# Moving the products of v's sums with w_in behind the output product in an attention and ELU layer kernel

## The chip, the cores and the metric

The kernel runs on one core of one Trainium2 chip. The metric is the device time of one execution in microseconds (us), as the median of the runs; lower is better.

## The reference

Two parts follow each other. The first is an attention with 32 memory slots: phi (8 batches, 8 heads, 576 positions, 32 slots) gives weights over positions, with which k and v are summed into 32 slots per head; q then attends to the slots. The second takes the result, 512 values for each of 4608 tokens, through w_in, an ELU and w_out.

```python
a = phi - np.max(phi, axis=2, keepdims=True)
a = np.exp(a)
a = a / (np.sum(a, axis=2, keepdims=True) + 1e-09)
k_m = np.einsum('bhsm,bhsd->bhmd', a, k)
v_m = np.einsum('bhsm,bhsd->bhmd', a, v)
...
scores = scale * np.matmul(q, k_m.transpose(0, 1, 3, 2))
...
attn = attn / (np.sum(attn, axis=-1, keepdims=True) + 1e-09)
return np.matmul(attn, v_m).astype(np.float32)
...
h = x @ w_in
g = np.where(h > 0.0, h, alpha * (np.exp(np.minimum(h, 0.0)) - 1.0))
return (g @ w_out).astype(np.float32)
```

The inputs are float32, w_in is 512 x 2048, w_out 2048 x 512.

## The kernel before, in words

The kernel never forms the attention's output. It multiplies v's sums of a batch with w_in first (`vw`, line 594), a small product per head, and then the probabilities A with that result. In the profile the product is line L502, which writes psb and reads win and kvm; L502 with qt in place of win is the score product. The product of one batch comes in four parts, one for each block of 512 columns of w_in; the text calls them the products with the first to the fourth block.

Each such product fills two accumulator banks named psb, of which there are two in all; the sums over positions (`slots`, L453), their transposes (`slots_transpose`, L487) and the scores use the same two in turn. ScalarE copies each bank as a high part into the tile vw (`vw_high`, L605), and VectorE writes the remainder as a low part (`vw_low`, L611). A bank is free once its low part is written.

The main loop runs over 256 steps `it`, each a batch b, a half hf of its positions (288) and a chunk j of 128 of the 2048 channels. A step has:

- `hidden` (L657, psh <- A, vw), six matmuls into one of two banks psh: the *channel product*;
- the ELU: two ScalarE passes (`elu_exp`, L672 and L673, into gf), and on VectorE the maximum (`elu_max`, L684, and L686 for the 32 rest columns), after which the psh bank is free;
- the split into a high part (`elu_high`, L698, ScalarE) and a low part (`elu_low`, L704, VectorE) in the tile gp;
- `project` (L712, pso <- wout, gp), six matmuls into two banks that collect a half's output over 16 chunks: the *output product*.

The channel product of a step stands two steps ahead of its output product. So TensorE's queue is channel product, output product, channel product, output product, and the work of the next batch's attention is placed in between.

The order is set by places: `at(place, f, ...)` records a step, and the list is sorted by place. `hidden` of step it has place it - 1.7, `project` it + 0.6, so between two whole steps n and n+1 the places are n + 0.3 for a channel product and n + 0.6 for an output product. For batches 2 to 7, `products(b, c, o)` (line 828) puts the product of batch b with block c at o, its high part at o + 0.75 and its low part at o + 0.76. `attention(b, o)` places the rest: phi's maximum and its way through DRAM to all partitions (`spread_max`, tiles nmd and nmb), the shift of e by it on GpSimd (`e_shift`, L289) and the exponential on ScalarE (`e_exp`, L294), the sums, their transposes at o + 7.2 and the copy of the transposes (`kv_copy`, L494, tile kvm). For batches 0 and 1 and the start of batch 2 the order is a table written out by hand (`FIRST`), which includes the products of batch 2 with its first two blocks. 22 products are left for the plan.

The recorded order is kept as it is on TensorE and for SyncE's transfers. On ScalarE, VectorE and GpSimd, outside the hand-written table, the framework's scheduler sets the order. All engines run their queues in order.

The batch's attention is placed against the batch ahead of it: the transposes of batch b's sums stand shortly behind the product of batch b-1 with its fourth block, and the shifts and exponentials of e of batch b shortly behind that of batch b-1 with its third block. When a pair of batches is done, the columns left over from the halves (288 = 2 x 128 + 32) are put through w_out together (`rest_project`, also L712, and the copy `rest_store`, L771).

## Time and profile before

| what | value |
|---|---|
| median of 3 runs | 736.43 us (736.42 to 736.93) |
| the profiled execution | 735.4 us, its span 733.6 us |
| TensorE matmul busy | 709.2 us of the span |
| VectorE busy | 467.2 us |
| ScalarE busy | 465.0 us |
| GpSimd busy | 44.6 us |
| mean granted TensorE clock | 0.990 |

The profile is one execution. Its times count from the first instruction. In rows of the timeline the first number is the start, the second the time from there to the end of the group, then the engine (PE is TensorE, PEld its weight loads, DVE VectorE, ACT ScalarE, POOL GpSimd, SP SyncE), the line of the kernel, the operation, what it writes and reads by the program's names, and in brackets how long the engine was idle just before and on what it waited. Matmuls overlap and their ends are modelled, so the time of a block of matmuls is read from its start to the start of the next block. A row may hold several instructions (x6).

### The profile page before, as it was taken

The page shows a single profiled execution, that of the slowest core. Times are in us where ns is not written, and L with a number is a line of the kernel's source. Part 1 is how long each engine was busy: PE and PEld are TensorE (multiplying, and loading weights), DVE is VectorE, ACT ScalarE, POOL GpSimd, SP SyncE. Part 2 cuts the span into 40 slices and gives each one's busy share as a digit, 9 for nine tenths or more (in the row PEclk, how much of TensorE's full clock was granted, in tenths as well). Part 3 has the DMA queues.
Part 4 walks back from the last instruction along what each step waited for, and adds up shares of the span by engine and source line. Part 5 has one row for each costly group of instructions (what it writes and reads, how often), then busy time and mean ns, then how long its engine had stood idle before and what let it go on. Part 6 is the DMA issues. An engine that isn't in the chain of part 4 may idle for free.

```text
span 733.6 us, 13668 instructions
## 1 busy us (share of the span) xinstructions
PE 709.2 (97%) x5114; PEld 572.5 (78%) x5114; DVE 467.2 (64%) x1253; ACT 465.0 (63%) x1110; POOL 44.6 (6%) x88
## 2 busy tenths in 40 slices
PE   7688999999999999999999999999999999999997
PEld 6566888888768878877788777887787887888885
DVE  4999899886495467544954449545774447754442
ACT  4768988886456656755655557656565565665552
POOL 0001112123000100010000100000000010000000
PEclk9899999999999999999999999999999999999999
DMA  8960513431316110611015210260002600010002
GB/s 311 370 231 28 203 30 115 149 101 62 101 59 210 28 44 1 239 42 45 2 57 182 56 45 1 75 206 28 18 1 75 218 27 20 1 58 0 2 1 72
DMA packets 24978, 64.46 MB, mean 88 GB/s; under 512 B 3408, under 2 KB 7632, under 8 KB 24912
## 3 DMA queue, kind: packets, MB, share of 16 engines
q1 hardware_dynamic: 24912, 63.59, 25.7%
q8 instruction: 41, 0.67, 0.4%
q14 instruction: 25, 0.20, 0.1%
HBM read 54.13 MB, written 9.44 MB: 87 GB/s over the span
## 4 chain that ended last, share of the span: by engine, by line
PE 68%; DMA 14%; DVE 8%; ACT 5%; issue 2%; POOL 1%; SPq 1%; POOLq 0%; DVEq 0%; ACTq 0%
PE pso L712 41%; PE psh L657 21%; DMA nmd<-nm 6%; PE psb L502 4%; DMA nmb<-nmd 3%; PE psb L453 2%; DMA ph<-phiT 2%; POOL e L289 1%; DMA win<-w_in 1%; ACT gf L673 1%; DMA kvt<-kv 1%; ACT gf L672 1%; DMA e<-phi 1%; DVE gf L681 1%; DVE nm L407 1%
## 5 line engine op out<-in xcount | busy, mean ns | idle before, releaser
L712 PE MATMUL pso<-wout,gp 128*128 128x512 f32 x1728 | 449.6, 398 | 3.3 <-DVE gp L704 2.6
L712 PEld LDWEIGHTS pso<-wout,gp 128*128 128x128 f32 x1728 | 310.1, 188 | 84.2 <-ACT gf L673 13.0
L657 PEld LDWEIGHTS psh<-A,vw 128*128 128x128 f32 x1536 | 229.9, 189 | 39.5 <-issue 6.2
L657 PE MATMUL psh<-A,vw 128*128 128x288 f32 x1536 | 251.1, 299 | 8.6 <-DVE rest L686 3.8
L684 DVE SCALAR_TENSOR_TENSOR gf<-gf,psh 128x256 f32<-128x256 f32 x192 | 80.4, 419 | 130.3 <-ACT gf L673 130.0
L672 ACT ACTIVATE gf<-psh 128x288 f32<-128x288 f32 x256 | 104.7, 409 | 86.3 <-PE psh L657 84.4
L698 ACT CAST gp<-gf 128x256 fp32r<-128x256 f32 x256 | 103.4, 404 | 87.0 <-DVE gf L684 73.4
L704 DVE TENSOR_TENSOR gp<-gf,gp 128x256 fp32r<-128x256 f32 x256 | 107.6, 421 | 55.0 <-ACT gp L698 54.7
L673 ACT ACTIVATE gf<-gf 128x288 f32<-128x288 f32 x256 | 113.7, 444 | 7.8
L611 DVE TENSOR_TENSOR vw<-psb,vw 128x512 fp32r<-128x512 f32 (+2 forms) x74 | 43.3, 602 | 11.7 <-ACT vw L605 11.5
L289 POOL TENSOR_TENSOR e<-e,nmb 128x512 f32<-128x512 f32 (+1 forms) x18 | 19.7, 1122 | 377.1 <-DMA nmb<-nmd 374.8
L681 DVE SCALAR_TENSOR_TENSOR gf<-gf,psh 128x288 f32<-128x288 f32 x64 | 28.9, 452 | 18.2 <-ACT gf L673 16.9
L605 ACT CAST vw<-psb 128x512 fp32r<-128x512 f32 (+2 forms) x74 | 37.1, 522 | 2.9 <-PE psb L502 0.7
L502 PE MATMUL psb<-win,kvm 64*32 64x512 f32 (+2 forms) x592 | 36.0, 541 | 0.0
L694 POOL COPY rest<-gf 128x32 f32<-128x32 f32 x64 | 24.3, 380 | 167.6 <-DVE gf L681 167.5
L686 DVE SCALAR_TENSOR_TENSOR rest<-gf,psh 128x32 f32<-128x32 f32 x192 | 34.2, 179 | 0.1
L752 ACT CAST gp<-rest 128x256 fp32r<-128x256 f32 x32 | 13.0, 406 | 23.8 <-PE pso L712 21.8
L373 DVE SCALAR_TENSOR_TENSOR top<-mag,top 128x512 uint32<-128x512 uint32 x32 | 22.2, 692 | 1.9 <-ACT mag L364 0.3
L757 DVE TENSOR_TENSOR gp<-rest,gp 128x256 fp32r<-128x256 f32 x32 | 13.4, 418 | 15.0 <-ACT gp L752 14.9
L368 ACT ACTIVATE mag<-raw 128x512 uint32<-128x512 uint32 x30 | 20.0, 670 | 2.5 <-DVE top L373 2.5
L294 ACT ACTIVATE e<-e 128x512 f32<-128x512 f32 (+1 forms) x18 | 9.8, 559 | 16.9 <-POOL e L289 16.8
L364 ACT ACTIVATE mag<-raw 128x512 f32<-128x512 f32 x30 | 19.5, 668 | 0.4 <-DVE win L385 0.4
(96 smaller groups left out, 368.4 us busy)
## 6 DMA issues: line engine op xcount, KB each, us to landing
kvt<-kv SPq DMA_DIRECT2D x32, 512.0 KB, 7.4
out<-osb SPq DMA_DIRECT2D x16, 512.0 KB, 2.8
raw<-w_in SPq DMA_DIRECT2D x15, 512.0 KB, 6.0
raw<-w_out SPq DMA_DIRECT2D x15, 512.0 KB, 7.9
qt<-q SPq DMA_DIRECT2D x18, 384.0 KB, 4.3
ph<-phiT SPq DMA_DIRECT2D x7, 576.0 KB, 5.0
e<-phi SPq DMA_DIRECT2D x12, 256.0 KB, 6.3
qh<-q SPq DMA_DIRECT2D x4, 576.0 KB, 11.5
```

The costliest lines, as they stand in the source:

```text
L502: nc.tensor.matmul(outs[a][32 * j : 32 * j + 32, :], lhs[r, 32 * j : 32 * j + 32], rhs[r, j], start=True, stop=True, tile_position=(64 * a ...
L605: nc.scalar.copy(s["vw"][c][:, HI, a, n0:n1], ps)
L611: nc.vector.tensor_tensor(t[:, LO, a, n0:n1], ps, t[:, HI, a, n0:n1], ALU.subtract)
L657: nc.tensor.matmul(ps, t[:, x, g, c0 : c0 + P], s["A"][hf][:, y, g, :], start=(n == 0), stop=(n == 5),)
L672: nc.scalar.activation(gf, ps, AF.Relu, scale=-1.0)
L673: nc.scalar.activation(gf, gf, AF.Exp, scale=-1.0)
L681: nc.vector.scalar_tensor_tensor(gf, gf, -1.0, ps, ALU.add, ALU.max)
L684: nc.vector.scalar_tensor_tensor(gf[:, :n], gf[:, :n], -1.0, ps[:, :n], ALU.add, ALU.max)
L686: nc.vector.scalar_tensor_tensor(rest_of(b, j)[:, o : o + REST], gf[:, n:], -1.0, ps[:, n:], ALU.add, ALU.max)
L698: nc.scalar.copy(gp[:, HI], gs[it][:, : NT * P])
L704: eng.tensor_tensor(gp[:, LO], gf[:, : NT * P], gp[:, HI], ALU.subtract)
L712: nc.tensor.matmul(ps, gp[:, y], wout[j][:, x, :], start=(first and n == 0), stop=(last and n == 2),)
```

## The change

One number in the plan: the place of the products of batches 2 to 7.

```diff
         attention(b, 43 if b == 2 else base - 22)
         for c in range(NVC):
-            products(b, c, base - 7.6 + 8 * c)
+            products(b, c, base - 7.35 + 8 * c)
```

`base` and 8c are whole numbers. Before, a product stood at a place n + 0.4: behind a channel product (n + 0.3) and ahead of an output product (n + 0.6). Now it stands at n + 0.65: behind that output product and ahead of the next channel product (n + 1.3). Its high and low parts move by the same 0.25, from n + 1.15 to n + 1.40 and from n + 1.16 to n + 1.41. The number of instructions and what they compute stay the same. The orders of SyncE and GpSimd are the same; those of TensorE, ScalarE and VectorE change.

## The prediction

> **What bounds the kernel now.** I read the page first: the busy shares.

> ```profile
> PE 709.2 (97%) x5114; PEld 572.5 (78%) x5114; DVE 467.2 (64%) x1253; ACT 465.0 (63%) x1110; POOL 44.6 (6%) x88
> ```

> TensorE is busy 97% of the span. So a microsecond that TensorE waits is a microsecond of time, and what VectorE and ScalarE do counts only where TensorE comes to wait for it. The change adds no instruction. It has to be priced by two things: what a change of neighbours costs on TensorE, and which waits appear or go.

> The timeline of TensorE alone gives the neighbours' prices: from one block's start to the next block's start is what a block costs. This stretch holds batch 4's product with the third block of w_in (L502, 16 records); L657 are channel products, L712 output products.

> ```profile
> 409.90 0.96 PE L657 MATMUL psh<-A,vw 128*128 128x288 f32 x6
> 410.79 1.09 PE L502 MATMUL psb<-win,kvm 64*32 64x512 f32 x16
> 411.81 1.65 PE L712 MATMUL pso<-wout,gp 128*128 128x512 f32 x6
> 413.30 0.96 PE L657 MATMUL psh<-A,vw 128*128 128x288 f32 x6
> 414.10 1.56 PE L712 MATMUL pso<-wout,gp 128*128 128x512 f32 x6
> 415.50 0.95 PE L657 MATMUL psh<-A,vw 128*128 128x288 f32 x6
> 416.29 0.43 PE L712 MATMUL pso<-wout,gp 128*128 128x512 f32 x1
> 417.02 1.42 PE L712 MATMUL pso<-wout,gp 128*128 128x512 f32 x5 [0.30 <-DVE gp L704]
> 418.95 1.04 PE L657 MATMUL psh<-A,vw 128*128 128x288 f32 x6 [0.51 <-DVE rest L686]
> ```

> An undisturbed channel block takes 0.80 us (413.30 to 414.10) and an output block 1.40 (414.10 to 415.50). With the product between them the channel block takes 0.89, the product 1.02, the output block 1.49. The second thing to see: here TensorE's close row of blocks breaks. The output block of 416.29 is followed by the next channel block only at 418.95, 2.66 us on, 1.26 more than undisturbed. ScalarE's timeline and GpSimd's over the same stretch tell why.

> ```profile
> 411.34 0.44 ACT L673 ACTIVATE gf<-gf 128x288 f32<-128x288 f32 x1
> 414.76 0.63 ACT L294 ACTIVATE e<-e 128x512 f32<-128x512 f32 x1 [2.98 <-POOL e L289]
> 415.30 0.57 ACT L605 CAST vw<-psb 128x512 fp32r<-128x512 f32 x1
> 415.76 0.41 ACT L698 CAST gp<-gf 128x256 fp32r<-128x256 f32 x1
> 416.07 0.59 ACT L605 CAST vw<-psb 128x512 fp32r<-128x512 f32 x1
> 416.55 0.94 ACT L294 ACTIVATE e<-e 128x512 f32<-128x512 f32 x2
> 417.38 0.40 ACT L672 ACTIVATE gf<-psh 128x288 f32<-128x288 f32 x1
> ```

> ```profile
> 413.42 3.26 POOL L289 TENSOR_TENSOR e<-e,nmb 128x512 f32<-128x512 f32 x3 [90.00 <-DMA nmb<-nmd]
> ```

> ScalarE waits 2.98 us for the first of GpSimd's three shifts of e, and everything behind it in its queue comes late: the casts, and then L672, which a channel block needs done before a later one may use its bank again.

> Then the list of who waited for whom (us in all, times, longest), the timeline of TensorE around batch 4's product with the fourth block of w_in, and VectorE's first low part there.

> ```profile
> PEld psb L487 <- DVE vw L611: 1.3, 5, 0.3
> ```

> ```profile
> 432.63 0.95 PE L657 MATMUL psh<-A,vw 128*128 128x288 f32 x6
> 433.51 1.09 PE L502 MATMUL psb<-win,kvm 64*32 64x512 f32 x16
> 434.53 1.66 PE L712 MATMUL pso<-wout,gp 128*128 128x512 f32 x6
> 436.02 0.42 PE L487 MATMUL psb<-ident,x 128*128 128x128 f32 x2
> 436.20 1.04 PE L657 MATMUL psh<-A,vw 128*128 128x288 f32 x6
> 437.08 1.56 PE L712 MATMUL pso<-wout,gp 128*128 128x512 f32 x6
> 438.57 0.56 PE L502 MATMUL psb<-qt,kvm 64*32 64x192 f32 x16
> 439.05 1.07 PE L657 MATMUL psh<-A,vw 128*128 128x288 f32 x6
> 439.97 1.29 PE L712 MATMUL pso<-wout,gp 128*128 128x512 f32 x5
> ```

> ```profile
> 435.26 0.69 DVE L611 TENSOR_TENSOR vw<-psb,vw 128x512 fp32r<-128x512 f32 x1 [0.21 <-ACT vw L605]
> ```

> Five times the weight load of the transposes (L487) waits for VectorE's L611, the low part of the product just before: the transposes write into the bank that L611 empties. Today that wait costs TensorE nothing. The product begins at 433.51, L611 ends at 435.95, the transposes start at 436.02, and until just then the output block (434.53 to 436.02) fills TensorE. That block is the cover.

> **The change, part by part.** All 22 products that the plan places keep their work; each moves behind the output block that followed it.

> (1) The product with the fourth block, five times (batches 2 to 6). TensorE's order at batch 2's, pso being output blocks, psh channel blocks, psb<-win the product, psb<-ident,x the transposes:

> ```order
>  L712 MATMUL pso_2849<-wout_1317,gp 128x512 x3
>  L657 MATMUL psh<-A,vw 128x288 x6
> -L502 MATMUL psb<-win_80,kvm 32x512 x8
>  L712 MATMUL pso_2825<-wout_1591,gp 128x512 x3
>  L712 MATMUL pso_2826<-wout_1591,gp 128x512 x3
> +L502 MATMUL psb<-win_80,kvm 32x512 x8
>  L487 MATMUL psb<-ident,x 128x128 x2
>  L657 MATMUL psh<-A,vw 128x288 x6
> ```

> The output block no longer stands between the product and the transposes, so the cover is gone and the wait is paid in full. From the product's start to the transposes' start it is 2.51 us (433.51 to 436.02), whichever block lies between: both halves must be cast by L605 and L611 before the first bank is free. Before, from the channel block to the next output block: 432.63 to 437.08, 4.45 us. After: channel block 0.80, output block ahead of a tiled product 1.49 (437.08 to 438.57), product and wait 2.51, transposes 0.18 and channel block 0.88 (436.02 to 437.08): 5.86. That is +1.41 each, +7.05 for five. Behind the waiting transposes stand the next channel block and all of TensorE's queue, so nothing fills the gap; ScalarE's and VectorE's ELU work runs dry with it. Bounds: at least 1.41 - 0.11 = 1.30 each if the joint behind the output block (1.49 against 1.40) and the transposes' cost nothing in the new place, at most 1.60 if a cast starts 0.2 late (6.5 to 8.0). L605 now stands behind L698, whose input is an ELU that ends before the product does, so I take no delay from it.

> (2) The product with the third block, five times (batches 2 to 6), where ScalarE waits for e. There the order of ScalarE's queue changes too. Batch 4's, before: L672 and L673 are the ELU's two passes, L698 the cast of its result, L294 the three exponentials of e, L605 the casts of the product.

> ```order
> L673 ACTIVATE gf<-gf 128x288
> L294 ACTIVATE e<-e 128x512
> L605 CAST vw<-psb 128x512
> L698 CAST gp<-gf 128x256
> L605 CAST vw<-psb 128x512
> L294 ACTIVATE e<-e 128x512
> L294 ACTIVATE e<-e 64x256
> L672 ACTIVATE gf<-psh 128x288
> ```

> And with the change:

> ```order
> L673 ACTIVATE gf<-gf 128x288
> L294 ACTIVATE e<-e 128x512 x2
> L698 CAST gp<-gf 128x256
> L294 ACTIVATE e<-e 64x256
> L605 CAST vw<-psb 128x512 x2
> L672 ACTIVATE gf<-psh 128x288
> ```

> The second exponential now stands ahead of L698 and of both casts, and GpSimd gives its input only at about 416.0: the first shift took 1.3 (413.42 to just before 414.76), and so does the second. So after the first exponential (414.76 to 415.39) ScalarE waits again: second exponential 416.03 to 416.66, L698 to 416.98, third exponential to 417.28, the casts L605 from 417.18 to 418.25, L672 from 418.15 where it was 417.38: +0.77. What follows L672 keeps its gaps, and the channel block of 418.95, which waits for the last of it, comes at 419.72. The output block of 416.29 goes on about 0.45 later than now, and ends before that: no further wait. So +0.77 here. Batches 2 and 6 have the same two exponentials ahead of the casts. In batches 3 and 5 the order is another: L672 and L673 stand between the exponentials, and the third exponential, L698 and both L605 ahead of the next L672, where one L605 stood on each side of the third exponential and L698. Batch 5's rows now, ScalarE alone:

> ```profile
> 496.83 0.42 ACT L673 ACTIVATE gf<-gf 128x288 f32<-128x288 f32 x1
> 497.16 0.56 ACT L605 CAST vw<-psb 128x512 fp32r<-128x512 f32 x1
> 497.62 0.41 ACT L294 ACTIVATE e<-e 64x256 f32<-64x256 f32 x1
> 497.94 0.39 ACT L698 CAST gp<-gf 128x256 fp32r<-128x256 f32 x1
> 498.24 0.58 ACT L605 CAST vw<-psb 128x512 fp32r<-128x512 f32 x1
> 498.71 0.41 ACT L672 ACTIVATE gf<-psh 128x288 f32<-128x288 f32 x1
> ```

> With the first cast moved behind L698, the third exponential takes its place at 497.16, and L698 starts at about 497.74 (VectorE's maximum, which it waits for, ends some 0.45 behind L673's end at 497.25). Then the casts at 498.05 and 498.53 and L672 at 499.02: +0.31, and the channel block that waits for it comes about 0.30 later. Sum: 3 x 0.77 + 2 x 0.30 = +2.9. Batches 2, 3 and 6 I take like the two that I worked out. Bounds: 0, if the delay of the exponentials is taken up somewhere behind, and 5 x 1.0, if every place costs batch 4's 0.77 and another 0.2 of a late cast.

> (3) The other 12 products. Before: 0.89 + 1.02 + 1.49 and a channel block of 0.80 behind, 4.20. After: channel 0.80, output 1.49, product 1.02, channel block behind a tiled product 0.91 (439.05 to 439.97, from the score product), 4.22. +0.02 each, +0.2. The casts L605 now follow L698 and precede the next L672; that one's input comes only after the later channel block, so they fit between, and no wait is added. One place needs a look: the product with a batch's second block now stands behind that batch's first output block, which writes a bank that has to be emptied first. The tightest case, behind the rest columns' output, ScalarE's copy and TensorE's channel block:

> ```profile
> 391.18 0.95 PE L657 MATMUL psh<-A,vw 128*128 128x288 f32 x6
> ```

> ```profile
> 391.38 0.59 ACT L771 COPY orest<-pso 128x512 f32<-128x512 f32 x1 [0.99 <-PE pso L712]
> ```

> The copy ends at 391.97, the channel block without its joint at 391.98. So the output block could wait 0.1 at most, at two places; I take nothing.

> SyncE's and GpSimd's orders are unchanged, so no DMA is moved.

> Sum: 7.05 + 2.9 + 0.2 = +10.2. The profiled execution took 735.4 us, its span 733.6; so 745.6 in its terms. The median of the runs shown is 1.0 above it, 736.43, so the forecast is 746.6.

> **Rivals.** (a) ScalarE's new order costs nothing, the transposes' wait is all: 736.4 + 7.2 = 743.7. It needs the exponentials' inputs to come earlier against TensorE; nothing on SyncE or GpSimd does that. Chance 0.10.

> (b) The channel block runs past the waiting transposes, so (1) costs nothing: 736.4 + 3.1 = 739.5. Against it: in the rows above TensorE's blocks start in the order in which they stand. Chance 0.04. [...]

> (c) Not slower: the stall in (2) vanishes altogether at all five places, because the maxima (nmb) land early enough that ScalarE never waits for e. Gain: 1.26 us at batch 4 as read above, so about 6.2 for five if the others are alike (an estimate from that row), against 7.05 + 0.2: 736.4 + 1.1 = 737.5, within what can be told from no change, and under it if the others were larger. It decides once GpSimd's first shift ends by 411.78, where L673 ends, and not just before 414.76: 3 us earlier. Against it: the transfers stand in SyncE's unchanged queue. Chance 0.06.

> (d) The five gaps of 1.5 us make the granted clock fall. The lowest granted clock of any stretch that I read is 0.81, near the start; behind the gap of batch 4 it is 1.00.

> ```profile
> 416.20:419.80 3.60, 2.79 (x14) 1.94 (x14) 2.31 (x6) 3.05 (x8) 0.49 (x1) 1.00 0.00 0
> 18.34:36.68 18.34, 12.38 (x179) 10.08 (x182) 17.72 (x50) 13.90 (x37) 0.42 (x2) 0.81 1.03 370
> ```

> If each gap cost what that stretch lost, 0.19 x 18.3 = 3.5 us, it would add up to 17: 764. Chance 0.03. [...]

> **The numbers.** The forecast has 0.77; its bounds are 736.4 + 6.5 = 742.9 and 736.4 + 8.0 + 5.0 + 0.4 = 749.8. The range 743.2 to 749.0 takes in (a) and leaves out (b), (c), (d) and the outermost of the bounds. A measurement of this kernel can tell about 0.2% (1.5 us) from no change. Of (c)'s 0.06, 0.04 lie within it and 0.02 under it; all else is slower: 0.94.

> **What would show it.** Right: the list of waits shows TensorE's transposes (psb, L487) waiting for VectorE's L611 at some 1.5 us five times; block starts show 2.5 us from each fourth product to its transposes; the e places show the channel block 0.8 (batches 2, 4, 6) or 0.3 us later behind the shifts; the other twelve places show 4.2 us. Wrong: L487 without a long wait, or the e places without a gap.

## The result and the profile after

The changed kernel takes 745.58 us (median of 6 runs, 743.80 to 749.13), the kernel before 735.89 (6 runs, 732.79 to 736.93): ratio 1.0145, 95% interval 1.0126 to 1.0165. That is +10.7 us by the ratio, +9.7 by the medians. (The ratio, here and below, is a figure of its own: it can differ from the quotient of the two medians by about 0.1%, which lies within its interval.) The profiled execution took 748.56 us, its span 746.8.

Page of the changed kernel, busy shares:

```profile
PE 712.0 (95%) x5114; PEld 572.0 (77%) x5114; DVE 468.8 (63%) x1253; ACT 466.2 (62%) x1110; POOL 44.5 (6%) x88
```

The instructions are the same in number. TensorE's busy time rose by 2.8 us, the span by 13.2, and its share fell from 97 to 95%. So most of the time went into waits. The list of waits of the changed kernel (us in all, times, longest):

```profile
ACT e L294 <- POOL e L289: 18.4, 11, 3.3
PEld psb L487 <- DVE vw L611: 11.6, 5, 2.3
PE psb L487 <- DVE vw L611: 7.0, 5, 1.4
PE psh L657 <- DVE rest L686: 6.1, 7, 2.0
```

The last of these rows before:

```profile
PE psh L657 <- DVE rest L686: 3.8, 5, 1.1
```

The transposes (L487) wait for the low part L611 five times, 7.0 us in all, 1.4 each: a wait that TensorE did not show before. The wait of the channel blocks for L686 was there; it grew from 3.8 us (5 times) to 6.1 (7 times). ScalarE's wait for e grew from 16.8 us to 18.4. The timelines of TensorE and VectorE at batch 4's product with the fourth block:

```profile
442.05 1.55 PE L712 MATMUL pso<-wout,gp 128*128 128x512 f32 x6
443.53 1.09 PE L502 MATMUL psb<-win,kvm 64*32 64x512 f32 x16
446.02 0.44 PE L487 MATMUL psb<-ident,x 128*128 128x128 f32 x2 [1.40 <-DVE vw L611]
446.22 1.04 PE L657 MATMUL psh<-A,vw 128*128 128x288 f32 x6
```

```profile
445.28 1.29 DVE L611 TENSOR_TENSOR vw<-psb,vw 128x512 fp32r<-128x512 f32 x2 [0.79 <-ACT vw L605]
```

From the product to its transposes it is 2.49 us, where it was 2.51, but the output block now stands ahead of the product and nothing fills the wait.

To see where the time comes, each of the 256 channel blocks of one trace is set beside the same block of the other, and the difference of their starts is followed through the program. Of the 13.16 us between the two profiled executions

- 2.6 arise before step 71, ahead of every product that was moved, while the inputs are loaded. TensorE's order is the same up to there in the traces of before, of the changed kernel and of experiments 1 to 5, and they reach step 70 between 227.4 and 230.6 us, the changed kernel's last. So this part is not the change's, and the profiled pair stands farther apart than the medians;
- 6.94 at the five fourth products: 1.39, 1.39, 1.38, 1.38, 1.39;
- 3.62 at the five third products, where ScalarE waits for e: 2.71, 0.33, 0.09, 0.20, 0.29 for batches 2 to 6 (each over ten steps around it);
- 0.03 at all other places together.

Batch 2's third product is the odd one. TensorE's timeline there, and two stretches of it (us, busy time of the engines, granted clock behind POOL's):

```profile
245.70 1.56 PE L712 MATMUL pso<-wout,gp 128*128 128x512 f32 x6
249.22 1.04 PE L657 MATMUL psh<-A,vw 128*128 128x288 f32 x6 [1.96 <-DVE rest L686]
250.10 2.65 PE L712 MATMUL pso<-wout,gp 128*128 128x512 f32 x6
252.54 1.45 PE L657 MATMUL psh<-A,vw 128*128 128x288 f32 x6
253.83 1.56 PE L712 MATMUL pso<-wout,gp 128*128 128x512 f32 x6
```

```profile
250.10:253.80 3.70, 3.70 (x14) 3.11 (x13) 1.89 (x6) 1.67 (x5) 0.00 (x0) 0.54 0.01 2
253.80:257.00 3.20, 3.20 (x19) 2.76 (x18) 0.94 (x3) 2.01 (x5) 0.00 (x0) 1.00 0.00 0
```

Behind a gap of 1.96 us the clock is granted at 0.54 for 3.7 us: the output block takes 2.44 (250.10 to 252.54) instead of 1.40, the next channel block 1.29 instead of 0.80, with no wait shown. That is 1.53 of the 2.71.

### The profile page after: what moved, and what is told of

It reads as the page before. It is cut to its first block, busy times and chain, and to the rows that moved or that the text cites. A ratio compares the mean times of both kernels' runs of the same rounds, so it can differ in the third digit from the quotient of the medians.

```text
span 746.8 us, 13660 instructions
## 1 busy us (share of the span) xinstructions
PE 712.0 (95%) x5114; PEld 572.0 (77%) x5114; DVE 468.8 (63%) x1253; ACT 466.2 (62%) x1110; POOL 44.5 (6%) x88
## 4 chain that ended last, share of the span: by engine, by line
PE 69%; DMA 12%; DVE 9%; ACT 5%; issue 2%; POOL 1%; SPq 1%; POOLq 0%; DVEq 0%; ACTq 0%
PE pso L712 41%; PE psh L657 21%; DMA nmd<-nm 5%; PE psb L502 4%; DMA nmb<-nmd 3%; PE psb L453 2%; DVE vw L611 2%; DMA win<-w_in 1%; DMA ph<-phiT 1%; ACT gf L673 1%; ACT vw L605 1%; POOL e L289 1%; ACT gf L672 1%; DMA kvt<-kv 1%; DMA e<-phi 1%
## 5 line engine op out<-in xcount | busy, mean ns | idle before, releaser
L712 PE MATMUL pso<-wout,gp 128*128 128x512 f32 x1728 | 448.5, 397 | 3.2 <-DVE gp L704 2.3
L712 PEld LDWEIGHTS pso<-wout,gp 128*128 128x128 f32 x1728 | 310.9, 189 | 66.5 <-DVE gp L704 3.6
L657 PEld LDWEIGHTS psh<-A,vw 128*128 128x128 f32 x1536 | 228.8, 189 | 54.4 <-issue 10.8
L657 PE MATMUL psh<-A,vw 128*128 128x288 f32 x1536 | 252.9, 300 | 10.9 <-DVE rest L686 6.1
L698 ACT CAST gp<-gf 128x256 fp32r<-128x256 f32 x256 | 103.3, 404 | 94.8 <-DVE gf L684 81.1
L684 DVE SCALAR_TENSOR_TENSOR gf<-gf,psh 128x256 f32<-128x256 f32 x192 | 80.4, 419 | 123.2 <-ACT gf L673 122.9
L672 ACT ACTIVATE gf<-psh 128x288 f32<-128x288 f32 x256 | 104.8, 410 | 80.3 <-PE psh L657 79.1
L704 DVE TENSOR_TENSOR gp<-gf,gp 128x256 fp32r<-128x256 f32 x256 | 107.6, 421 | 68.5 <-ACT gp L698 68.3
L673 ACT ACTIVATE gf<-gf 128x288 f32<-128x288 f32 x256 | 113.7, 444 | 7.8
L611 DVE TENSOR_TENSOR vw<-psb,vw 128x512 fp32r<-128x512 f32 (+2 forms) x74 | 42.0, 603 | 15.7 <-ACT vw L605 15.0
L289 POOL TENSOR_TENSOR e<-e,nmb 128x512 f32<-128x512 f32 (+1 forms) x18 | 19.6, 1117 | 386.0 <-DMA nmb<-nmd 292.5
L605 ACT CAST vw<-psb 128x512 fp32r<-128x512 f32 (+2 forms) x74 | 35.3, 521 | 11.6 <-PE psb L502 11.6
L502 PE MATMUL psb<-win,kvm 64*32 64x512 f32 (+2 forms) x592 | 35.8, 538 | 0.3 <-DVE win L385 0.3
L686 DVE SCALAR_TENSOR_TENSOR rest<-gf,psh 128x32 f32<-128x32 f32 x192 | 34.1, 178 | 0.1
L294 ACT ACTIVATE e<-e 128x512 f32<-128x512 f32 (+1 forms) x18 | 10.0, 558 | 18.4 <-POOL e L289 18.4
```

Of the source, the lines that this page charges most:

```text
L502: nc.tensor.matmul(outs[a][32 * j : 32 * j + 32, :], lhs[r, 32 * j : 32 * j + 32], rhs[r, j], start=True, stop=True, tile_position=(64 * a ...
L605: nc.scalar.copy(s["vw"][c][:, HI, a, n0:n1], ps)
L611: nc.vector.tensor_tensor(t[:, LO, a, n0:n1], ps, t[:, HI, a, n0:n1], ALU.subtract)
L657: nc.tensor.matmul(ps, t[:, x, g, c0 : c0 + P], s["A"][hf][:, y, g, :], start=(n == 0), stop=(n == 5),)
L672: nc.scalar.activation(gf, ps, AF.Relu, scale=-1.0)
L673: nc.scalar.activation(gf, gf, AF.Exp, scale=-1.0)
```

## The experiments

**Theory**: each fourth product costs about 1.4 us, because its transposes need the bank that its low part empties and no block is left in between; each third product costs some tenths, because ScalarE's queue has the casts and L672 behind more exponentials of e than before; the other products cost nothing. **Rivals**: the cost lies in the new neighbours on TensorE or ELU casts that come late at every product; or ScalarE's order costs nothing and the transposes' wait is all.

**1. The fourth products alone.** Only c == 3 is moved, all else as before.

```diff
-            products(b, c, base - 7.6 + 8 * c)
+            products(b, c, base - (7.35 if c == 3 else 7.6) + 8 * c)
```

> The product with the fourth block alone stands behind the output block, the other three stand where they stood before. Theory (the transposes wait for the bank that the product's low part empties): from the fourth product's start to the transposes' start 2.5 us at five places, TensorE's blocks there +1.4 each, +7.0 us over before in all, and ScalarE's order at the shifts of e as before, so no change there. Rival (the time comes from the product's new neighbours at all 22 places, 10.6 us / 22 = 0.5 each): 6 products moved, +2.9.

Measured: 738.48 us, the kernel before 732.31 on that chip; ratio 1.0081 (1.0059 to 1.0103), +5.9 where +7.0 was expected, which lies within the interval; the rival's +2.9 does not. Its trace against that of before has the step 1.39, 1.39, 1.39, 1.38, 1.39 at the five places. Its list of waits has the same row for PE's L487 as that of the full change, 7.0 us, 5 times, 1.4 at the longest: the wait belongs to the fourth product alone.

**2. All but the fourth.** The condition turned round (`7.6 if c == 3 else 7.35`).

> The first three products are moved as in the change, the fourth stands where it stood before. Theory (two separate costs: the transposes' wait at the fourth, ScalarE's order at the third): no wait at the transposes; at the shifts of e +3 to +4 us in all over five places, the most of it in batch 2; together +3 to +4 over before. Rival (cost of the new neighbours, 0.5 at each of 22 places): 16 products moved, +7.7.

Measured: 735.20, ratio 1.0030 (1.0010 to 1.0049), +2.2, less than the +3 to +4 expected and far from the rival's +7.7. TensorE's fourth places cost 0.00. The third products took 0.5 us more than in the trace of before; why one trace says little here is told further down.

**3. The transposes into another bank.** The full change, but the transposes of batches 3 to 7 write a psh bank instead of a psb bank; so they don't wait for L611.

```diff
-        at(o + 7.2, slots_transpose, b)
+        at(o + 7.2, slots_transpose, b, *(((0, 1), "h") if b > 2 else ()))
```

> As changed, but the transposes of batches 3 to 7 write into a bank of the channel products (psh) in place of one that the product has just filled. TensorE's order is the same. Theory (wait for the bank): the transposes start 1.0 to 1.1 us behind the product's start in place of 2.5, so 7 us less than changed, +3 to +4 over before. Rival (the step from the tiled product to full-array transposes itself costs 1.5 us): the gap stays, +10 to +11 over before.

Measured: 734.18, ratio 1.0028 (1.0012 to 1.0043), +2.1, again under the +3 to +4 expected. TensorE at batch 4:

```profile
433.16 1.55 PE L712 MATMUL pso<-wout,gp 128*128 128x512 f32 x6
434.64 1.09 PE L502 MATMUL psb<-win,kvm 64*32 64x512 f32 x16
435.67 0.44 PE L487 MATMUL psh<-ident,x 128*128 128x128 f32 x2
435.86 1.04 PE L657 MATMUL psh<-A,vw 128*128 128x288 f32 x6
```

The transposes follow the product after 1.03 us. The product stands where the change put it, and the five steps of +1.39 are gone (now -0.09 each: the joint between product and transposes costs nothing, where that between product and output block had cost 0.09). So this wait is the bank's, and the new neighbours don't make it.

**4. Half a cover.** The full change, and the transposes one block later, behind the next channel block.

```diff
-        at(o + 7.2, slots_transpose, b)
+        at(o + 7.35, slots_transpose, b)
```

> As changed, but the transposes of batches 3 to 7 stand behind the next channel block, so that this block (0.9 us) lies between product and transposes. Theory (wait for the bank, 2.5 us from the product's start whatever lies between): a wait of 2.5 - 1.0 - 0.9 = 0.6 is left at five places, and one joint more of 0.1; 3.5 to 4.3 us less than changed, +6 to +7 over before. Rival (a fixed cost of having the product behind the output block): as changed, +10 to +11.

Measured: 737.32, ratio 1.0064 (1.0041 to 1.0086), +4.7, under the +6 to +7 expected. What was expected of experiments 2 to 4 is what the profiled pair's 3.62 us at the third products would give, and that pair was high. TensorE at batch 4:

```profile
436.03 1.09 PE L502 MATMUL psb<-win,kvm 64*32 64x512 f32 x16
437.05 1.07 PE L657 MATMUL psh<-A,vw 128*128 128x288 f32 x6
438.53 0.44 PE L487 MATMUL psb<-ident,x 128*128 128x128 f32 x2 [0.41 <-DVE vw L611]
```

Product to transposes is 2.50 again; the channel block covers part of it, and the places cost 0.60, 0.61, 0.59, 0.60, 0.59. With a cover of an output block 0, of a channel block 0.6, of nothing 1.39: the bank is free some 2.5 us behind the product's start in all three, and what stands in between decides how much of it shows.

**5. The first two products alone** (`7.6 if c > 1 else 7.35`): the neutral part.

> The products with the first and second block alone are moved (10 of 22). Theory (a moved product is neutral where no wait is added): +0.2 us, no change that can be told. Rival (0.5 us at each moved product): +5.

Measured: 731.79 beside 732.71, ratio 0.9996 (0.9983 to 1.0008). No cost that can be told, as the theory has it; the rival's +5 is out.

**6 to 8. Shifts of e that come earlier: an attempt that failed.** To see whether ScalarE's wait for e goes once the maxima land early, phi's load, maximum and way through DRAM were placed 8 steps earlier; in the kernel before, in the changed one, and in the changed one with the other bank of experiment 3.

```diff
-        at(o - 4, load_phi, b)
+        at(o - 12, load_phi, b)
...
-        at(o + 0.1, phi_max, b)
+        at(o - 8.1, phi_max, b)
...
-            at(o + 0.12, phi_exp, b, g)
+            at(o - 8, phi_exp, b, g)
...
-        at(o + 1, spread_max, b)
+        at(o - 7, spread_max, b)
```

> The kernel before, with phi's load, its maximum, its sums and the maxima's way through DRAM planned some 8 steps earlier, ahead of the loads of k and v. The products stand as before. Theory (TensorE's breaks behind the third product come from ScalarE waiting for GpSimd's shifts of e, and those for the maxima): the maxima land 5 us or more earlier, the five breaks of 0.7 to 1.4 us go, -5 to -6 us against before. Rival (the breaks come from the three exponentials' own time on ScalarE, 0.4 to 0.6 us each): they stay, 0 to -1.

> The changed kernel with the same earlier maxima. Theory (the change's second cost is the order of ScalarE's queue while it waits for e): without that wait only the transposes' wait is left, +7 over the kernel before with earlier maxima, +1 to +2 over before. Rival (the moved third product costs by itself): +10 to +11 over the kernel before with earlier maxima, +4 to +6 over before.

> The changed kernel with earlier maxima and with the transposes of batches 3 to 7 in a channel bank. Theory (two waits and nothing else): both costs gone, as fast as the kernel before with earlier maxima or up to 0.5 us faster (one joint less at five places), -5 to -6.5 us against before. Rival (22 moved products cost something of their own): slower than that by some microseconds, 0 to -3 against before.

Measured: 763.76 (ratio 1.0435, 1.0415 to 1.0455), 761.75 (1.0414, 1.0383 to 1.0446) and 754.68 (1.0315, 1.0298 to 1.0331), the kernel before 732.71 beside them. All three miss. SyncE's queue of the first of the three and its wait for e:

```profile
304.47 0.46 SPq L276 DMA_DIRECT2D nmd<-nm  x1
309.81 0.34 SPq L278 DMA_DIRECT2D nmb<-nmd  x1
310.25 0.38 SPq L300 DMA_DIRECT2D kvt<-kv  x1
310.72 0.38 SPq L267 DMA_DIRECT2D e<-phi  x1
```

```profile
POOL e L289 <- DMA e<-phi: 312.4, 11, 96.2
```

nmb has to wait for nmd on its way through DRAM, 5.3 us, and now the loads of kv and e stand behind it in SyncE's queue: GpSimd waits for e itself, hardly any more for the maximum. ScalarE's order of the exponentials moved as well, and its wait for e grew from 16.8 to 24.7 us. So this experiment changed the wait, and says nothing on the question it was made for. One pair is still of use: the other bank takes 7.1 us off the second of these kernels, as it took the wait away in experiment 3.

**9 to 11. ScalarE in the recorded order.** Another way to the same question: ScalarE's queue, too, is kept in the order of the places, so no exponential of e stands ahead of a cast that is placed before it. The casts' offset of the products becomes 0.5 (0.75 before). This was done to the kernel before, to the changed one, and to the changed one with the other bank.

```diff
-    with tc.manual_schedule(engines={mybir.EngineType.PE, mybir.EngineType.SP}):
+    with tc.manual_schedule(engines={mybir.EngineType.PE, mybir.EngineType.SP, mybir.EngineType.Activation}):
...
-        at(o + (0.3 if cols else 0.75), vw_high, b, c, *cols)
-        at(o + (0.31 if cols else 0.76), vw_low, b, c, *cols)
+        at(o + (0.3 if cols else 0.5), vw_high, b, c, *cols)
+        at(o + (0.31 if cols else 0.51), vw_low, b, c, *cols)
```

> The kernel before, its products where they stood, with ScalarE's queue kept in the order of the plan too (the casts of a product ahead of the ELU's next cast). Each exponential of e then stands one step apart and about 3.5 steps behind the third product, where GpSimd's shift should be done. Theory (TensorE's breaks behind the third product are ScalarE waiting at the head of its queue for the shifts): the breaks go, -4.5 to -6 us against before. Rival (ScalarE has too much to do there, the order does not matter): they stay, 0 to -1.

> The changed kernel with ScalarE's queue in the order of the plan (the casts' places kept where they were before the change, which puts them ahead of the next ELU). The transposes still write into the product's bank. Theory (the change costs the transposes' wait, 7 us, and the rest through the order while ScalarE waits for the shifts): +6.5 to +7.3 over the kernel before with ScalarE in the plan's order, +1 to +2.5 over before. Rival (the moved third product costs 3 us by itself): +10 to +11 over that kernel, +4 to +6 over before.

> The changed kernel with ScalarE in the plan's order and the transposes of batches 3 to 7 in a channel bank. Theory (two waits and nothing else): within 0.5 us of the kernel before with ScalarE in the plan's order, -5 to -6.5 against before. Rival (22 moved products cost something of their own): 2 us or more slower than that kernel.

Measured, the kernel before 732.11 beside them: 737.57 (1.0077, 1.0052 to 1.0102), 740.83 (1.0128, 1.0105 to 1.0151), 733.69 (1.0021, 1.0010 to 1.0032). ScalarE and TensorE around batch 4's third product, in the changed kernel with this order:

```profile
416.10 1.07 ACT L605 CAST vw<-psb 128x512 fp32r<-128x512 f32 x2 [0.64 <-PE psb L502]
417.09 0.41 ACT L672 ACTIVATE gf<-psh 128x288 f32<-128x288 f32 x1
```

```profile
413.49 1.56 PE L712 MATMUL pso<-wout,gp 128*128 128x512 f32 x6
414.97 1.09 PE L502 MATMUL psb<-win,kvm 64*32 64x512 f32 x16
415.99 1.06 PE L657 MATMUL psh<-A,vw 128*128 128x288 f32 x6
```

No wait for e, no break, and between the first two kernels of this group the third products cost 0.0 and the fourth 1.39 each. So the cost at the third products hangs on ScalarE's queue. But the totals of all three were misses. Experiment 9 is +5.6 us where -4.5 to -6 was expected: the five breaks at e are gone (5.9 us together in the trace of before, but only 2.9 and 2.1 in those of experiments 1 and 5), and new ones stand in their place, five of 1.16 or 1.17 us at the first product and three of 0.9, 0.5 and 0.4 elsewhere. ScalarE and TensorE of experiment 9, batch 4's rows:

```profile
459.33 0.51 ACT L584 CAST A<-pr 128x384 fp32r<-128x384 f32 x1 [1.65 <-DVE pr L567]
459.75 1.07 ACT L605 CAST vw<-psb 128x512 fp32r<-128x512 f32 x2
460.70 0.41 ACT L698 CAST gp<-gf 128x256 fp32r<-128x256 f32 x1
```

```profile
459.93 0.96 PE L657 MATMUL psh<-A,vw 128*128 128x288 f32 x6
461.17 0.50 PE L712 MATMUL pso<-wout,gp 128*128 128x512 f32 x1 [0.28 <-ACT gp L698]
462.04 1.43 PE L712 MATMUL pso<-wout,gp 128*128 128x512 f32 x5 [0.36 <-DVE gp L704]
```

In the recorded order a cast of the probabilities (L584) waits for VectorE's L567 at the head of the queue, with the casts L605 and L698 behind it. With the products in the changed place L605 goes behind L698, and each of these breaks shrinks by 0.71: here the change helps. That is why experiment 10 stands only 3.3 us above experiment 9 (five times 1.39 less five times 0.71), not the 6.5 to 7.3 expected, and experiment 11 stands 3.9 under it, where it was expected within 0.5 of it.

**12. Both waits gone, and the casts of A later.** Experiment 11 with L584 and its low part placed 0.65 later, behind that L698.

```diff
-        at(o + 5 * step, probs_high, b, u)
-        at(o + 6 * step, probs_low, b, u)
+        at(o + 5 * step + 0.65, probs_high, b, u)
+        at(o + 6 * step + 0.65, probs_low, b, u)
```

> The version with both waits gone still shows TensorE breaking once in each of five batches: where the product with the first block stands, the output block takes 1.85 us instead of 1.40, because VectorE's low part L704 comes late: ScalarE's cast L698 ahead of it stands behind a cast of A (L584), which waits for VectorE's L567. Here the casts of A and their low parts are placed 0.65 later, behind that L698. Theory (the queue order on ScalarE alone makes that break): the five output blocks fall back to about 1.49, that is -0.36 to -0.45 each, together -1.8 to -2.2 us against the version with both waits gone (732.1 us span beside it, 733.69 by the median of its runs, 1.4 above the kernel before on its chip); so 0.9975 to 1.000 of the kernel before. Rival (the later A is waited for by the low parts of A and by the softmax of the next tile on VectorE, whose queue then delays L684): the same five breaks move a step on, no gain: ratio 1.001 to 1.003 as before.

Measured: 730.99 (12 runs) beside 731.82 (17 runs); ratio 0.9985 (0.9973 to 0.9997). That is within what was expected. Against experiment 11's trace the five places give -0.45 each. ScalarE at the first of them, batch 3's first product:

```profile
283.67 0.41 ACT L698 CAST gp<-gf 128x256 fp32r<-128x256 f32 x1 [0.50 <-DVE gf L684]
284.81 0.51 ACT L584 CAST A<-pr 128x384 fp32r<-128x384 f32 x1 [0.74 <-DVE pr L567]
285.23 1.07 ACT L605 CAST vw<-psb 128x512 fp32r<-128x512 f32 x2
```

L584 still waits, 0.74, but behind the cast that TensorE needs. With the products in the changed place, the other bank and the two new orders on ScalarE this is a version slightly under the kernel before, by 1.1 us, close to the least that can be told.

## Why the prediction came out as it did

The forecast was 746.6 us, +10.2; measured 745.58, +9.7 by the medians and +10.7 by the ratio (the kernel before stood at 736.43 in the forecast and at 735.89 with the later runs). Step by step:

**(1) The transposes' wait: right.** +1.41 each, +7.05 in all; measured 1.39 and 6.94. It goes with the bank (experiment 3), it is there with the fourth product alone (1), and it shrinks to 0.6 under half a cover (4). Rival (a) holds as far as this wait goes, but the third products cost something as well, so it isn't all. Rival (b), a channel block that passes the waiting transposes, is out: the transposes start at 446.02 after their wait of 1.40, the channel block behind them at 446.22.

**(2) ScalarE's order at the third product: the cost of the order right, the arrival of e left out.** Forecast +0.77, +0.30, +0.77, +0.30, +0.77 for batches 2 to 6, 2.9 in all; the profiled pair shows 2.71 (1.53 of it clock), 0.33, 0.09, 0.20, 0.29, 3.62 in all. That these two sums are near each other is in part luck, as the single batches show. Experiments 2 and 3, where this term stands nearly alone, give +2.2 and, with the 0.46 of the saved joints added back to 0.28% of 732.3, +2.5. The working behind the 0.77 is borne out. ScalarE in the changed kernel at batch 4 (before: 414.76 to 417.38), then at batch 2, then at batch 2 in the kernel before:

```profile
422.64 0.63 ACT L294 ACTIVATE e<-e 128x512 f32<-128x512 f32 x1 [2.32 <-POOL e L289]
...
426.01 0.41 ACT L672 ACTIVATE gf<-psh 128x288 f32<-128x288 f32 x1
```

```profile
244.58 0.63 ACT L294 ACTIVATE e<-e 128x512 f32<-128x512 f32 x1 [2.48 <-POOL e L289]
...
247.65 0.39 ACT L672 ACTIVATE gf<-psh 128x288 f32<-128x288 f32 x1
```

```profile
241.66 0.63 ACT L294 ACTIVATE e<-e 128x512 f32<-128x512 f32 x1 [1.99 <-POOL e L289]
...
243.95 0.39 ACT L672 ACTIVATE gf<-psh 128x288 f32<-128x288 f32 x1
```

From the first exponential to L672 it was 2.62 us at batch 4 and is 3.37, +0.75; at batch 2, 2.29 and 3.07, +0.78. It is the same in every trace in which the scheduler sets ScalarE's order and the maxima stand where they stood: three with the third product in its old place (before, experiments 1 and 5), four with it moved (the changed kernel, experiments 2 to 4). The time in us from the first exponential to the L672 behind the third one, least and most:

| third product | batch 2 | batch 3 | batch 4 | batch 5 | batch 6 |
|---|---|---|---|---|---|
| old place | 2.29 to 2.50 | 3.69 to 3.70 | 2.63 | 3.69 to 3.70 | 2.63 |
| moved | 3.06 to 3.26 | 3.97 to 3.99 | 3.35 to 3.37 | 3.98 to 3.99 | 3.35 to 3.36 |

So the order alone costs some 0.74, 0.29, 0.73, 0.29 and 0.73, 2.8 in all, and the forecast's 2.9 is right for it.

The step that failed is the one left unsaid in "+0.77 here": that GpSimd's first shift comes at the same time against TensorE's blocks. Measured from the start of the same channel block (before 240.16 and 413.30, after 242.62 and 421.74), the first exponential comes 0.46 later at batch 2 (1.50, now 1.96) and 0.56 earlier at batch 4 (1.46, now 0.90). So batch 2 pays 0.78 + 0.46 = 1.24 ahead of the clock's fall, and batch 4 0.75 - 0.56 = 0.19, each less 0.09 for the joint that the channel block ahead no longer has: 1.15 and 0.10, where the steps show 1.18 and 0.09.

GpSimd waits there for the maximum's second transfer (nmb), not for TensorE. Over the seven traces the first exponential of one batch comes 1.0 to 1.4 us apart against the same channel block. SyncE issues the first transfer (nmd) at nearly the same time against that block, within 0.1 us at batch 2 and within 0.7 at the others; from this issue to the landing of nmb it takes 10.9 to 13.6 us, 1.0 to 1.6 apart at one batch. So most of the scatter arises in the two transfers; what makes them longer or shorter isn't shown. It is as large as the term itself. Against experiments 9 to 12, which have no wait at e in these places, nine steps around each of the five third products together took 5.9, 2.9 and 2.1 us longer in the three traces with the old place, and 9.7 (1.5 of it clock), 6.5, 4.8 and 4.4 in the four with the move. The means differ by 2.7, by 2.3 without the clock, which agrees with the forecast; one pair of traces alone could not show it.

**(3) The other twelve: right.** +0.2 forecast; 0.03 at all other places in the trace, and a ratio of 0.9996 for the first two products alone.

**Rival (c), no stall at e**: the list of waits still has 18.4 us. The version that the rival describes, a wait that vanishes, exists only under ScalarE's recorded order (experiments 9 to 11), with its price elsewhere. **Rival (d), the clock**: happened, but not at the five gaps that it named. None of those cost any clock (1.00 in the 2 us behind each); the gap of 1.96 us at batch 2 did, 1.53 us in the one trace. In the traces of experiments 2, 3 and 4, whose third products stand in the changed place too, the gap at batch 2 was 0.85, 1.11 and 0.86 us, and the clock stayed at 1.00: so this loss is no fixed part of the change. Whether the other executions of the changed kernel have it isn't known. The two halves measured apart, 0.81% and 0.30%, add up to 1.11%, the full change to 1.45%: the difference, 0.34%, is about as large as the intervals together allow (the root of the sum of their squares is 0.35%), so what it is made of stays open, the clock among the candidates.

## What to carry to other kernels

Where two users of one accumulator bank follow each other on TensorE, read the time from the first one's start to the bank's release (here 2.5 us: product, two casts, two low parts) and look what stands between them: a block of 1.4 us hid all, one of 0.8 more than half, none nothing. A plan that only moves an instruction by one place moves such covers, and also the order of queues that a scheduler fills; price both, and where the second hangs on a transfer, give the arrival a range, since it does not follow TensorE: here it scattered by 1.0 to 1.4 us from trace to trace, and only several traces together showed the cost of the order.

## What the runs showed of the hardware that was not expected

All figures here were measured in the traces of this case's own runs: TensorE's busy time and the granted clock, by stretches of the span.

A longer gap on TensorE did not always cost more clock. In the changed kernel at batch 2, behind the gap of 1.96 us, the clock was granted at 0.50 from 250.23 to 253.64 us, which cost the 1.53 us, and at 1.00 in the rows ahead of it and behind it:

```profile
246.82:250.23 3.41, 1.45 (x9) 1.04 (x8) 2.23 (x5) 2.83 (x8) 0.00 (x0) 1.00 0.00 0
250.23:253.64 3.41, 3.41 (x12) 2.82 (x11) 1.89 (x6) 1.56 (x4) 0.00 (x0) 0.50 0.01 2
253.64:257.06 3.42, 3.42 (x20) 2.98 (x19) 0.94 (x3) 2.07 (x5) 0.00 (x0) 1.00 0.02 5
```

In experiment 7 a gap of 2.16 us cost nothing: 0.65 us of it lie in the first of these rows and 1.52 in the second, and all three stood at 1.00.

```profile
260.74:264.15 3.41, 2.76 (x25) 1.32 (x23) 1.34 (x3) 1.85 (x4) 0.00 (x0) 1.00 0.33 128
264.15:267.57 3.42, 1.90 (x12) 1.77 (x13) 2.49 (x6) 2.82 (x8) 0.00 (x0) 1.00 0.00 0
267.57:270.98 3.41, 3.41 (x32) 2.46 (x31) 2.62 (x8) 1.57 (x4) 0.00 (x0) 1.00 0.00 0
```

Other gaps, with the clock in the 2 us from 0.3 us behind them:

- the five gaps of 1.4 us at the fourth products, in the changed kernel and in experiments 1 and 10: 1.00 behind all fifteen;
- in experiment 6, 2.50 us (up to 318.70) and 2.54 us (up to 354.66): 0.94 and 0.50; in experiment 7, 2.53 us (up to 418.30): 0.50.

In experiment 6 the clock fell behind two short gaps as well, 0.84 us up to 233.03 and 0.98 us up to 234.51, 1.82 us together: 0.85 from 234 to 236 us, 0.50 to 238, 0.79 to 240.

The two sets of rows are told apart by the idle time in one row, 1.96 us against 1.52, and not by the length of the gap, 1.96 us against 2.16. That the idle time in such a row is what counts is the author's reading; what sets the clock isn't shown, and no run was made to test it.
